# Two elementwise steps of an attention and feed-forward kernel on Pool instead of DVE

## The chip, the cores and the metric

The kernel runs on one core of one Trainium2 chip. The metric is device time in microseconds (us) of one execution; shorter is better. The engines of a core are named as the profile names them: PE multiplies matrices (PEld is its weight load), DVE and Pool (POOL) and ACT work elementwise, SP only issues DMAs here. Each engine takes its instructions in the order in which they stand in its own queue, and waits for the others through semaphores.

## What is computed

The first half is attention with a mask from hash buckets, for 4 batches of 8 heads, 768 positions, head size 64; the second half is a gated convolution with two matrix products, on the heads joined to 512 channels:

```python
q_bits = (einsum('bhsd,dk->bhsk', q, proj) > 0)          # 6 bits a position, k likewise
mask   = q_bucket[:, :, :, None] == k_bucket[:, :, None, :]
scores = where(mask, scale * (q @ k.T), -1e9)
attn   = softmax(scores)
x      = (attn @ v)  # heads joined: [4, 768, 512]
for k in range(5):
    gate_pre += conv_w[k] * xp[:, k:k + 768, :]           # xp: x with 4 zeros in front
out = (sigmoid(gate_pre) * (x @ w_val)) @ w_out
```

All arrays are fp32 (the weights of the second half arrive as 64-bit floats and are taken apart on the chip).

## The kernel before, in words

A unit is one head of one batch: 32 units. A tile is 128 queries of a unit against its 768 keys: 6 tiles a unit, 192 tiles in all. The main loop `for k in range(N + LAG + 1)` takes one tile a step and writes, by hand, the order in which each engine gets its work: PE, ACT, DVE and Pool run exactly in the order in which the code issues it (`tc.manual_schedule`), and SP's order follows from that.

For tile k, `scores` multiplies queries with keys on PE in two passes that add up: the first with operands rounded to the fp32r format (`aq`, `ak`), the second with the remainders (`bq`, `bk`). `maxima` takes the negated row maximum `nm` on DVE, `factors` and `shifts` make the two small columns `gs` and `nb`, and `exponentials` turns the scores to `p` on ACT with the row sums. For two tiles at a time `row_sums` and `recip` make the reciprocals `ri`, and `normalise` multiplies `p` with them on Pool. `transposes` (PE, tiles `tp`), `keep_transposed` (ACT, `pt`) and `attn_v` (PE, `av`) follow up to four steps later.

The raw queries and keys `r` of a unit lie stacked in one 128x768 tile. `prep` makes the four operands of the next unit, in two steps of the loop: first the rounding cast `aq<-r` (line 166), a step later the remainder `bq<-r,aq` on Pool (line 168) and six DMAs on SP's queue that place halves of `aq`, `bq` and the bit rows `u` in `ak`, `bk`, `bq` and `aq`. `stk` holds two buffers of each, so a unit is prepared while the one ahead is worked on.

When two heads (a pair, 128 channels) have their `x`, `pair_x` splits it in `xh` (DVE cast) and `xl` (Pool subtraction), and then runs the five taps of the convolution, one a call: tap 0 writes `g` (line 332), taps 1 to 4 add to it (line 334, DVE, two tensors in). Up to step 60 it is called every other step, after that every step. Four pairs end in the sigmoid on ACT and a `moe` generator for the two matrix products (PE lines 365 and 390, DVE lines 370 and 374, Pool line 376).

Over about the first 180 us two generators `load_weights` also take the 64-bit weights apart, eight pieces of 128x512, each some six DVE instructions (lines 92 to 108), two on Pool (110, 112), one on ACT (90) and a DMA.

Of the kernel before, what the change touches and what calls it, by code (L numbers as in the profile page):

```python
# [11 lines left out]
ALU = mybir.AluOpType  # L12
# [14 lines left out]
def kernel(  # L27
# [10 lines left out]
    nc = tc.nc  # L38
    B, H, _, S = qk.shape
# [103 lines left out]
    def load_raw(i):  # L143
        if i < len(units):
            b, h = units[i]
            raws[i] = raw.tile([P, S], FP32, name="r")
            nc.sync.dma_start(out=raws[i], in_=qk[b, h])

    def load_values(i):
        b, h = units[i]  # L150
        if h % 2 == 0:
            vts[i] = vp.tile([P, KB, P], FP32, name="vt")
            nc.sync.dma_start(out=vts[i], in_=v[b, h // 2])
        else:
            vts[i] = vts[i - 1]

    def prep(i):

        if i >= len(units):
            return  # L160
        b, h = units[i]
        j = h % 4
        load_values(i)
        r = raws[i]
        aq, ak, bq, bk = stacks[i] = [stk.tile([P, S], FP32R, name=nm) for nm in ("aq", "ak", "bq", "bk")]
        nc.vector.tensor_copy(out=aq, in_=r)  # L166
        yield
        nc.gpsimd.tensor_tensor(out=bq, in0=r, in1=aq.bitcast(FP32), op=ALU.subtract)  # L168
        nc.sync.dma_start(out=ak[0:D].bitcast(FP32), in_=aq[D:P].bitcast(FP32))
        nc.sync.dma_start(out=bk[0:D].bitcast(FP32), in_=aq[D:P].bitcast(FP32))  # L170
        nc.sync.dma_start(out=bk[D:P].bitcast(FP32), in_=bq[D:P].bitcast(FP32))
        nc.sync.dma_start(out=bq[D:P].bitcast(FP32), in_=aq[0:D].bitcast(FP32))
        u = cur["u"]
        nc.sync.dma_start(out=aq[D:M].bitcast(FP32), in_=u[32 * j:32 * j + 2 * NB].bitcast(FP32))
        nc.sync.dma_start(out=ak[D:M].bitcast(FP32), in_=u[32 * j + 2 * NB:32 * j + 4 * NB].bitcast(FP32))
        load_raw(i + 5)
        if j == 3 and i + 1 < len(units):
            yield
            yield from bits(i + 1)
# [6 lines left out]
    def bits(i):  # L186

        u = stk.tile([P, S], FP32R, name="u", bufs=2)
        for hf in range(2):
            yield  # L190
            sl = slice(hf * HS, (hf + 1) * HS)
            z = side_tile()
            for jj in range(4):
                nc.tensor.matmul(out=z[32 * jj:32 * jj + 32, 0:HS], lhsT=proj_sb,
                                 rhs=raws[i + jj][:, sl], start=True, stop=True,
                                 tile_position=(0, 32 * jj))
            nc.vector.tensor_scalar(out=u[:, sl], in0=z[:, 0:HS], scalar1=rows_sb[:, 0:1], scalar2=rows_sb[:, 1:2],
                                    op0=ALU.is_ge, op1=ALU.mult)
        cur["u"] = u
# [94 lines left out]
    def attn_v(i, pts):  # L294
        b, h = units[i]
        hh, c = h % 2, h // 2
        av = ps_v.tile([P, 512], FP32, name="av")
        vt = vts[i]
        for kb in range(KB):
            if kb:  # L300
                yield
            for s, pt in enumerate(pts):
                nc.tensor.matmul(out=av[s * D:(s + 1) * D, 0:HS], lhsT=vt[:, kb, hh * D:(hh + 1) * D], rhs=pt[kb // 3][:, kb % 3, :],  # L303
                                 start=(kb == 0), stop=(kb == KB - 1), tile_position=(0, s * D))
        if hh == 0:
            x = cur["x"] = xp.tile([P, S + KW - 1], FP32, name="x")
            nc.gpsimd.memset(x[:, 0:KW - 1], 0.0)
        x = cur["x"]
        for s in range(2):
            o = KW - 1 + s * HS  # L310
            nc.scalar.copy(out=x[hh * D:(hh + 1) * D, o:o + HS], in_=av[s * D:(s + 1) * D, 0:HS])  # L311
        if hh == 1:
            if c == 0:
                cur["xs"], cur["g"] = {}, []
            convs.append(pair_x(b, c, x, cur["g"], cur["xs"]))

    def pair_x(b, c, x, gs, xs_):
        for o in (0, HS):
            xh = xs.tile([P, HS], FP32R, name="xh")
            xl = xs.tile([P, HS], FP32R, name="xl")  # L320
            xs_[(c, o)] = (xh, xl)
            x0 = x[:, KW - 1 + o:KW - 1 + o + HS]
            nc.vector.tensor_copy(out=xh, in_=x0)  # L323
            nc.gpsimd.tensor_tensor(out=xl, in0=x0, in1=xh.bitcast(FP32), op=ALU.subtract)  # L324
        yield
        g = gp.tile([P, S], FP32, name="g")
        gs.append(g)
        for k in range(KW):
            yield
            w = cw_sb[:, c * KW + k:c * KW + k + 1]  # L330
            if k == 0:
                nc.vector.tensor_scalar(out=g, in0=x[:, 0:S], scalar1=w, scalar2=None, op0=ALU.mult)
            else:
                nc.vector.scalar_tensor_tensor(out=g, in0=x[:, k:k + S], scalar=w, in1=g, op0=ALU.mult, op1=ALU.add)  # L334
        if c == NP - 1:
            yield
            for g in gs:
                nc.scalar.activation(out=g, in_=g, func=AF.Sigmoid)
            cur["gates"] = 2
            moes.append(moe(b, xs_, gs))  # L340
# [101 lines left out]
    with tc.manual_schedule(engines=ENGINES):  # L442
# [3 lines left out]
        first_prep()  # L446
        weights = [[load_conv(), load_weights(0)], [load_weights(1)]]
        preps = [first_bits(), prep(1)]
        scores(0)
        step(weights[0])  # L450
        step(weights[1])
        turn = 0
        for k in range(N + LAG + 1):
# [15 lines left out]
            if k + 1 < N:  # L469
                if tiles[k + 1][0] != tiles[k][0]:  # L470
                    finish(preps)
                    preps = [prep(tiles[k + 1][0] + 1)]
                scores(k + 1)
# [83 lines left out]
```

## Time and profile before

| what | value |
|---|---|
| time, median of 3 runs | 639.09 us (638.87 to 639.24) |
| the profiled execution | 637.56 us, span of its instructions 635.6 us |
| PE busy | 590.1 us (93%) |
| DVE busy | 465.9 us (73%) |
| ACT busy | 421.7 us (66%) |
| POOL busy | 364.7 us (57%) |

Busy time of an engine is the time in which the profile shows an instruction running on it. The shares are means over a span with three stages: up to about 200 us the weights are taken apart and there is no feed-forward work for PE, then comes the long middle, and after 580 us only feed-forward products are left. In the rows, a group reads: line, engine, operation, output<-inputs, shapes, count, busy time and mean duration of one, then the time the engine idled just before them and what ended it.

### The profile page before, as it was taken

Reading aid. Unit: us, or ns where it says so; the run is one execution under the profiler, and the core shown is the slowest. Engines: PE = TensorE matmul, PEld = TensorE weight load, DVE = VectorE, ACT = ScalarE, POOL = GpSimd, SP = SyncE. Lnnn points to the kernel's source line nnn. Section 1 sums busy time; section 2 is a strip of 40 time slices with the busy share of each in tenths; the row PEclk is TensorE's granted clock in tenths of the full one; section 3 lists DMA queues with packets and bytes.
Section 4 is the critical chain, followed back from the end, with each engine's and each line's share of the span. In section 5 each row is a group of like instructions: output and inputs, shape, how many; then the busy total and the mean of one; then the engine's idle time right before and its main releaser. Section 6 shows DMA issues by size and latency. Waiting matters only on the chain.

```text
span 635.6 us, 10630 instructions
## 1 busy us (share of the span) xinstructions
PE 590.1 (93%) x3496; PEld 424.3 (67%) x3496; DVE 465.9 (73%) x1064; ACT 421.7 (66%) x881; POOL 364.7 (57%) x326
## 2 busy tenths in 40 slices
PE   4689888878999999999999999999999999999997
PEld 2465554555567777676667877677667777776895
DVE  5789897999986766668675877578685787665532
ACT  3487776767778666667787766677778677675400
POOL 1375868577765764567653776466562677544221
PEclk9899998998999999999999999999999999999999
DMA  6533535443332334343433333343422223300111
GB/s 243 128 101 86 139 96 138 112 134 81 104 80 58 83 75 123 82 105 96 104 80 79 88 80 110 80 121 80 120 57 61 57 53 79 86 18 2 50 51 50
DMA packets 23269, 56.76 MB, mean 89 GB/s; under 512 B 4296, under 2 KB 4296, under 8 KB 23216
## 3 DMA queue, kind: packets, MB, share of 16 engines
q1 hardware_dynamic: 23072, 56.06, 32.9%
q8 instruction: 28, 0.46, 0.3%
q14 instruction: 25, 0.20, 0.1%
q10 hardware_dynamic: 144, 0.03, 0.0%
HBM read 23.12 MB, written 6.29 MB: 46 GB/s over the span
## 4 chain that ended last, share of the span: by engine, by line
PE 64%; DVE 18%; ACT 10%; issue 3%; DMA 3%; POOL 0%; DVEq 0%; ACTq 0%
PE av L303 16%; PE s L232 15%; PE tp L280 12%; PE m L390 8%; PE m L365 7%; DVE nm L238 6%; ACT p L256 4%; DVE g L334 3%; ACT pt L289 3%; ACT x L311 2%; DMA w<-in_w_out_dram 2%; DVE aq L166 1%; PE tp L365 1%; PE tp L390 1%; PE s L390 1%
## 5 line engine op out<-in xcount | busy, mean ns | idle before, releaser
L271 POOL TENSOR_SCALAR p<-p,ri 128x768 f32<-128x768 f32 x192 | 220.0, 1150 | 200.3 <-DVE nb L248 157.6
L256 ACT ACTIVATE p<-s,nb,gs 128x768 f32<-128x768 f32 x192 | 192.7, 1004 | 49.7 <-DVE nb L248 44.6
L289 ACT COPY pt<-tp 128x384 f32<-128x384 f32 x384 | 166.2, 485 | 86.0 <-PE tp L280 85.0
L238 DVE TENSOR_REDUCE nm<-s 128x1 f32<-128x768 f32 x192 | 182.4, 950 | 52.8 <-PE s L232 52.6
L280 PEld LDWEIGHTS tp<-ident,p 128*128 128x128 f32 x1152 | 130.4, 142 | 74.2 <-issue 47.3
L280 PE MATMUL tp<-ident,p 128*128 128x128 f32 x1152 | 165.4, 280 | 4.5 <-ACT pt L289 1.6
L232 PE MATMUL s<-ak,aq 76*128 76x384 f32 x384 | 118.6, 390 | 32.2 <-ACT p L256 25.4
L303 PE MATMUL av<-pt,vt 128*64 128x384 f32 x768 | 146.9, 504 | 0.0
L232 PE MATMUL s<-bk,bq 128*128 128x384 f32 x384 | 101.6, 346 | 0.0
L232 PEld LDWEIGHTS s<-ak,aq 76*128 76x128 f32 x384 | 59.4, 195 | 48.9 <-ACT p L256 39.3
L303 PEld LDWEIGHTS av<-pt,vt 128*64 128x64 f32 x768 | 47.4, 137 | 63.3 <-issue 62.7
L334 DVE SCALAR_TENSOR_TENSOR g<-x,cw_sb,g 128x768 f32<-128x768 f32 x64 | 78.4, 1225 | 0.2
L232 PEld LDWEIGHTS s<-bk,bq 128*128 128x128 f32 x384 | 71.9, 194 | 0.5 <-issue 0.5
L376 POOL TENSOR_TENSOR hl<-ht,hh 128x384 fp32r<-128x384 f32 x32 | 33.4, 1044 | 45.5 <-DVE hh L374 45.5
L168 POOL TENSOR_TENSOR bq<-r,aq 128x768 fp32r<-128x768 f32 x31 | 58.4, 1885 | 0.5 <-DVE aq L166 0.5
L311 ACT COPY x<-av 64x384 f32<-64x384 f32 x64 | 30.4, 475 | 33.5 <-PE av L303 32.9
L365 PE MATMUL m<-xh,wv 128*128 128x384 f32 x200 | 42.7, 337 | 0.0
L248 DVE TENSOR_SCALAR nb<-nm,gs 128x1 f32<-128x1 f32 x192 | 40.1, 209 | 3.5
L370 DVE TENSOR_TENSOR ht<-m,g 128x384 f32<-128x384 f32 x25 | 13.9, 555 | 35.4 <-PE m L365 32.0
L256 ACT ACTIVATION_READ_ACCUMULATOR p<-s,nb,gs 128x1 f32 x192 | 39.1, 204 | 0.0
L324 POOL TENSOR_TENSOR xl<-x,xh 128x384 fp32r<-128x384 f32 x32 | 33.5, 1066 | 9.5 <-DVE xh L323 9.5
L390 PE MATMUL m<-wo,hh 128*128 128x512 f32 x144 | 38.1, 394 | 0.0
(84 smaller groups left out, 475.6 us busy)
## 6 DMA issues: line engine op xcount, KB each, us to landing
r<-in_qk_dram SPq DMA_DIRECT2D x32, 384.0 KB
vt<-in_v_dram SPq DMA_DIRECT2D x16, 384.0 KB
out_dram<-o SPq DMA_DIRECT2D x24, 256.0 KB
ak<-aq SPq DMA_DIRECT2D x31, 192.0 KB
bk<-aq SPq DMA_DIRECT2D x31, 192.0 KB
bk<-bq SPq DMA_DIRECT2D x31, 192.0 KB
bq<-aq SPq DMA_DIRECT2D x31, 192.0 KB
w<-in_w_val_dram SPq DMA_DIRECT2D x4, 512.0 KB
```

The lines of the kernel that those rows point to most:

```text
L168: nc.gpsimd.tensor_tensor(out=bq, in0=r, in1=aq.bitcast(FP32), op=ALU.subtract)
L232: nc.tensor.matmul(out=s[:, hf, 0:HS], lhsT=lq[0:n, qs], rhs=rk[0:n, hf * HS:(hf + 1) * HS], start=n == M, stop=n == P)
L238: nc.vector.tensor_reduce(out=nm, in_=s[:, :, 0:HS], axis=AX.XY, op=ALU.max, negate=True)
L256: nc.scalar.activation(out=p, in_=s[:, :, 0:HS], func=AF.Exp, bias=nb, scale=gs.pop(k), accum_out=sm[:, k % 2, 0:1])
L271: nc.gpsimd.tensor_scalar(out=p, in0=p, scalar1=rcs.pop(k), scalar2=1.0, op0=ALU.mult, op1=ALU.mult)
L280: nc.tensor.transpose(out=tp[:, n * P:(n + 1) * P], in_=p[:, kb * P:(kb + 1) * P], identity=ident)
L289: nc.scalar.copy(out=pt[:, :, qo:qo + P], in_=tp[:, 0:HS].rearrange("p (a b) -> p a b", b=P))
L303: nc.tensor.matmul(out=av[s * D:(s + 1) * D, 0:HS], lhsT=vt[:, kb, hh * D:(hh + 1) * D], rhs=pt[kb // 3][:, kb % 3, :], start=(kb == 0), s ...
L311: nc.scalar.copy(out=x[hh * D:(hh + 1) * D, o:o + HS], in_=av[s * D:(s + 1) * D, 0:HS])
L334: nc.vector.scalar_tensor_tensor(out=g, in0=x[:, k:k + S], scalar=w, in1=g, op0=ALU.mult, op1=ALU.add)
L365: nc.tensor.matmul(out=acc[:, 0:HS], lhsT=wv[wi][:, c, j * P:(j + 1) * P], rhs=xs_[(c, o)][xi], start=(m == 0), stop=(m == 11))
L390: nc.tensor.matmul(out=acc, lhsT=hs[(o, j)][hi][:, tb * P:(tb + 1) * P], rhs=wo[wi][:, j, :], start=(m == 0), stop=(m == 11))
```

## The change

The rounding cast `aq<-r` of every unit but the first (31 times, 128x768) and the first tap `g` of every pair (16 times, 128x768) are issued on Pool instead of DVE. On Pool the tap is a multiplication by the weight column and then by 1.0, which is the form that `normalise` has there.

```diff
-        nc.vector.tensor_copy(out=aq, in_=r)
+        nc.gpsimd.tensor_copy(out=aq, in_=r)
...
-                nc.vector.tensor_scalar(out=g, in0=x[:, 0:S], scalar1=w, scalar2=None, op0=ALU.mult)
+                nc.gpsimd.tensor_scalar(out=g, in0=x[:, 0:S], scalar1=w, scalar2=1.0, op0=ALU.mult, op1=ALU.mult)
```

The order on PE and ACT stays as it was. Below, `-` is a row of before, `+` one of now, and the brackets name the engines and DMA queues whose semaphores an instruction waits for.

DVE, at the place that the trace of before shows at 75 to 81 us (unit 5's cast, while the weight piece `w_848` is taken apart):

```order
 L92 TENSOR_SCALAR o<-o 128x512 [waits Activation_49]
 L93 TENSOR_SCALAR o<-o 128x512 [waits DVE_49]
-L166 CAST aq<-r 128x768 [waits DMAHW4_49,DMAHW1_49,DMAHW5_49,DMAHW0_49,Pool_49]
 L238 TENSOR_REDUCE nm<-s 128x1 [waits PE_49]
 L262 TENSOR_SCALAR s_973<-sm 128x2 [waits Activation_49]
```

The row maximum of the next tile now stands directly behind the weight's instruction. The first tap leaves DVE in the same way a few rows on, and the second tap, line 334, gets a wait for Pool.

Pool, at the same place (`p` is the normalising of a tile, `w_516` a weight piece):

```order
 L271 TENSOR_SCALAR p<-p,ri 128x768 [waits PE_49,Activation_49]
 L112 TENSOR_TENSOR wv_119<-w_516 128x512 [waits Pool_49]
-L271 TENSOR_SCALAR p<-p,ri 128x768 [waits DVE_49,PE_49,Activation_49]
-L168 TENSOR_TENSOR bq<-r,aq 128x768 [waits DMAHW1_49,PE_49]
-L271 TENSOR_SCALAR p<-p,ri 128x768 [waits PE_49,Activation_49]
+L166 CAST aq<-r 128x768 [waits DMAHW4_49,DMAHW1_49,DMAHW5_49,DMAHW0_49,PE_49]
+L271 TENSOR_SCALAR p<-p,ri 128x768 [waits DVE_49,Activation_49]
+L168 TENSOR_TENSOR bq<-r,aq 128x768 [waits PE_49,Pool_49]
+L271 TENSOR_SCALAR p<-p,ri 128x768 [waits PE_49,Activation_49]
+L332 TENSOR_SCALAR g<-x,cw_sb 128x768
 L307 MEMSET x 128x4
 L271 TENSOR_SCALAR p<-p,ri 128x768 [waits DVE_49,PE_49,Activation_49]
```

The cast stands ahead of the first `p` of a pair of tiles and waits for PE; the tap stands behind the second `p`.

Pool, at the start (unit 1, 19 to 25 us):

```order
 L271 TENSOR_SCALAR p<-p,ri 128x768 [waits DVE_49,Activation_49,Pool_49]
+L166 CAST aq<-r 128x768 [waits DMAHW2_49]
 L271 TENSOR_SCALAR p<-p,ri 128x768 [waits Activation_49]
-L168 TENSOR_TENSOR bq<-r,aq 128x768 [waits DMAHW2_49,DVE_49]
+L168 TENSOR_TENSOR bq<-r,aq 128x768 [waits Pool_49]
 L271 TENSOR_SCALAR p<-p,ri 128x768 [waits DVE_49,Activation_49]
```

Here the cast falls between two `p`, so that one of these stands between the cast and the remainder. On SP's queue some of the small DMAs `aq<-u` move ahead of the loads of `r` and `vt` that stood in front of them.

## The prediction

> **What bounds the kernel now.** The page's busy times (PE 93%, DVE 73%) are a mean over different programs, so I read them by stage, the weights' conversion apart. Columns: the stretch, its length, then PE, PEld, DVE, ACT, POOL busy (instructions), granted clock, DMA share, GB/s.
>
> ```profile
> 20.00:200.00 180.00, 156.03 (x934) 104.46 (x935) 159.85 (x357) 133.69 (x285) 120.84 (x105) 0.96 0.41 107
> 200.00:580.00 380.00, 373.22 (x2270) 273.37 (x2270) 272.13 (x651) 272.22 (x571) 226.43 (x202) 1.00 0.32 82
> 580.00:636.00 56.00, 50.47 (x257) 41.23 (x254) 22.58 (x35) 10.00 (x17) 14.00 (x14) 1.00 0.11 43
> ```
>
> From 200 to 580 us PE is idle for 6.8 of 380 us: whatever leaves DVE there can hardly shorten anything. From 20 to 200 us PE idles 24.0 us and DVE is the fullest engine, 159.85 of 180. There the chain of waits runs through DVE. Its shares from 20 to 200 us, and pieces in order of time (start, us, what), among them those that the change removes:
>
> ```profile
> by line: DVE nm L238 16.6%; PE s L232 9.1%; issue 7.9%; PE av L303 7.6%; DMA w<-in_w_out_dram 5.9%; ACT p L256 5.9%; DVE g L334 5.3%; PE tp L280 4.6%; DVE aq L166 4.3%; DVE w L100 3.5%; DVE nb L248 3.1%; ACT pt L289 2.6%; DVE gs L244 2.6%;
> ...
> 20.54 1.05 DVE aq L166
> ...
> 80.91 1.68 DVE g L332
> ...
> 94.17 0.47 DVE aq L166
> ...
> 103.52 6.17 DMA w<-in_w_out_dram
> ...
> 115.76 1.68 DVE g L332
> ...
> 139.55 4.47 DMA w<-in_w_out_dram
> ...
> 146.75 1.39 DVE aq L166
> ...
> 177.66 0.94 DVE aq L166
> 179.91 0.54 DVE g L332
> ```
>
> The casts are 4.3% of 180 us, 7.74 us in ten pieces, of which the fence has the first, the last and two between; the taps are the three shown, 3.90 us. Together 11.64 us of the chain.
>
> **The change part by part.** The groups that it moves, and those beside which they come to stand:
>
> ```profile
> L271 POOL TENSOR_SCALAR p<-p,ri 128x768 f32<-128x768 f32 x192 | 220.0, 1150 | 200.3 <-DVE nb L248 157.6
> L168 POOL TENSOR_TENSOR bq<-r,aq 128x768 fp32r<-128x768 f32 x31 | 58.4, 1885 | 0.5 <-DVE aq L166 0.5
> L166 DVE CAST aq<-r 128x768 fp32r<-128x768 f32 x31 | 20.6, 665 | 0.2
> L332 DVE TENSOR_SCALAR g<-x,cw_sb 128x768 f32<-128x768 f32 x16 | 13.2, 827 | 0.0
> ```
>
> DVE loses 33.8 us of work. Pool gains 16 taps in exactly the form of `p`, 1150 ns each, 18.4 us, and 31 casts. No row has a Pool cast. The bounds are `p` (one tensor in, one out) at 1150 and `bq` (two in, one out, same rounded type) at 1885 ns; I take `p`, because `bq` reads twice as much, and allow the other end: 36 to 58 us. So Pool goes to 419 to 442 us of 636, and it has 200.3 us of idle ahead of `p` alone.
>
> 1. *Removed from the chain, 20 to 200 us.* The first piece (1.05) does not count, see 3. That leaves 10.6 us. Where DVE would next wait for PE, the gain is given back:
>
> ```profile
> 177.14 0.62 PE L232 MATMUL s<-ak,aq 76*128 76x384 f32 x2 [0.25 <-ACT p L256]
> 118.94 0.85 PE L194 MATMUL m<-r,proj_sb 128*32 128x384 f32 x8
> 120.31 0.67 DVE L197 TENSOR_SCALAR u<-m,packed 128x384 fp32r<-128x384 f32 x1
> ```
>
> At 177 us PE has a gap of only 0.25 us, so of the last two pieces (1.48) about 0.5 remains. At 120 us DVE's `u` needs the product that ends at 119.8, 0.5 us ahead of it, while the tap just before gave 1.68: some 1.1 us is lost. Gain 10.6 - 1.0 - 1.1 = 8.5 us.
>
> 2. *The matmul clock.* Two long waits of PE in this stage are followed by slow matmuls (eight of `av` take 1.51 us elsewhere, as at 134.08):
>
> ```profile
> 97.17 0.62 PE L232 MATMUL s<-ak,aq 76*128 76x384 f32 x2 [2.16 <-ACT p L256]
> 98.36 2.83 PE L303 MATMUL av<-pt,vt 128*64 128x384 f32 x8
> 150.69 0.61 PE L232 MATMUL s<-ak,aq 76*128 76x384 f32 x2 [2.08 <-ACT p L256]
> 151.58 2.20 PE L303 MATMUL av<-pt,vt 128*64 128x384 f32 x8
> 133.19 0.61 PE L232 MATMUL s<-ak,aq 76*128 76x384 f32 x2 [2.21 <-ACT p L256]
> 134.08 1.51 PE L303 MATMUL av<-pt,vt 128*64 128x384 f32 x8
> ```
>
> Gaps of 2.16 and 2.08 us cost 1.32 and 0.69 us in `av`; one of 2.21 us cost nothing. The casts at 94.17 and 146.75 lie in the first two waits; without them those shrink. Of 2.0 us I take half, 1.0: the first is followed by a weight's DMA that does not come sooner for it.
>
> 3. *The start.* Unit 1's operands run in series: cast, `bq`, DMAs, first scores at 28.06. Now one more `p` stands between cast and `bq`:
>
> ```profile
> 19.35 1.83 POOL L271 TENSOR_SCALAR p<-p,ri 128x768 f32<-128x768 f32 x2 [12.12 <-DVE nb L248]
> 20.46 1.14 DVE L166 CAST aq<-r 128x768 fp32r<-128x768 f32 x1
> 21.68 1.80 POOL L168 TENSOR_TENSOR bq<-r,aq 128x768 fp32r<-128x768 f32 x1 [0.50 <-DVE aq L166]
> 28.06 0.98 PE L232 MATMUL s<-ak,aq 76*128 76x384 f32 x2 [2.31 <-issue]
> ```
>
> First `p` to about 20.3, cast to 21.3, second `p` to 22.2: `bq` starts at 22.2 instead of 21.68, a loss of 0.5 us. The DMAs on SP keep their order there.
>
> 4. *New collisions of DVE and Pool.* The two hold each other up, whole instructions long. The cast that met `L112` took 1.39 us, the one with Pool idle 0.55; line 334 beside `L110` took 1.85:
>
> ```profile
> 76.07 1.20 POOL L112 TENSOR_TENSOR wv<-w 128x512 fp32r<-128x512 f32 x1
> 76.30 1.39 DVE L166 CAST aq<-r 128x768 fp32r<-128x768 f32 x1
> 94.09 0.55 DVE L166 CAST aq<-r 128x768 fp32r<-128x768 f32 x1
> 161.83 1.31 POOL L110 TENSOR_TENSOR w<-w,wo 128x512 f32<-128x512 f32 x1
> 162.10 1.85 DVE L334 SCALAR_TENSOR_TENSOR g<-x,cw_sb,g 128x768 f32<-128x768 f32 x1
> L334 DVE SCALAR_TENSOR_TENSOR g<-x,cw_sb,g 128x768 f32<-128x768 f32 x16 | 21.0, 1312 | 0.0
> ...
> L334 DVE SCALAR_TENSOR_TENSOR g<-x,cw_sb,g x64: 1006/1009/2339, 86.8 to 596.0; 128x768 f32<-128x768 f32 x64
> ```
>
> The stage's 16 taps of line 334 average 1.31 us where an undisturbed one takes 1.01 (the last row: shortest, median, longest): 4.8 us lost beside 120.84 us of Pool work, 0.04 us per us, and I double that for DVE's other instructions. The stage gets 12 casts and 4 taps of 1.15 us, 18.4 us: 1.5 us. The far bounds are a gain of 1.5, should the collisions of the removed instructions have cost Pool as much, and a loss of 18.4 us, if each new one stops DVE for its whole length. I take 3.0 us, more than the mean rate, because the cast falls into the stretch where DVE goes from the maximum to the weights' two-tensor instructions.
>
> The Trainium skill ("SBUF — State Buffer", Who interferes with whom) says this as a rule: a DVE instruction in a two-port mode or with two SBUF inputs and a Pool instruction that reads SBUF take one pair of ports as an exclusive lock, and the second waits in full. The trace agrees (0.55 against 1.39 us). By the rule a Pool instruction that DVE runs into costs the rest of its length, half of 1.15 us on the mean: were all 16 run into, this term would be 9.2 us and the sum -0.3 instead of -6.5. "GPSIMD Engine Reference" (Engine selection) advises VectorE for elementwise work, calling Pool about twice as slow with two inputs and near line rate with one; 665 against 1150 ns (the latter for `p`) lies between.
>
> 5. *200 us to the end.* The casts (11.4 us) and taps lie beside PE. The chain has two casts there:
>
> ```profile
> 320.62 0.47 DVE aq L166
> 466.64 0.47 DVE aq L166
> ```
>
> The second tap now waits for Pool's first, but Pool has a step for it (192 tiles in 580 us: 3.0 us). With some collisions, net gain 0.5 us.
>
> 6. *SP.* The queue waits for the cast anyway, with the remainder behind it later still; both move with `p`, and the operands are due more than four steps on. The moved `aq<-u` DMAs cost nothing for the same reason. If that cover went, the scores of a new unit would wait.
>
> Sum: -8.5 - 1.0 + 0.5 + 3.0 - 0.5 = -6.5 us. Against the profiled execution, 637.56 us (span 635.6 and 1.96 around it), that is 631.1; this execution lies 1.5 us under the median of the runs, 639.09, so I forecast **632.6 us**.
>
> **The rivals.**
> - *A clean gain.* The collisions wash out (those of the removed instructions go as well) and both clock losses vanish: -10.6 - 2.0 + 0.5 = -12.1, 627.0 us. For it: Pool idles 200.3 us ahead of `p`, where the casts can lie while DVE reads scores from PSUM. Against it: the gap of 0.25 us, where PE is next.
> - *Given back.* At 103 and 139 us the chain hangs on weight DMAs of 6.17 and 4.47 us, and PE's three lines have 21.3% of it; if these set the stage's length, DVE's relief is idle time: 638.5 to 640 us. Against it: PE's 24 us of idle in the stage, DVE's 20.
> - *Slower: the lock.* One new Pool instruction ahead of the reciprocal or of a two-tensor instruction stops the column that ACT's next exponential waits for. At 1.0 us for each of the 16 the loss is 16.0 against a gain of 10.0 - 0.5: +6.5, 645.6 us. It decides from a mean of 0.6 us each; at half of 1.15 us each, 9.2 us in all, it takes the whole gain (638.8 us), which stands with the 0.10 of "given back" below. Against it: of 16 taps of line 334 the mean loss is 0.3.
> - *Slower: a Pool cast beyond `bq`'s price.* At 3 us, cast, two `p` and `bq` fill 7.2 us of the 6.0 us that two steps take, and transposes wait: about 1 us a unit after 200 us, where nothing hides it, 20 us, less the gain: 652 us. Only an unknown rate speaks for it; `bq`'s rounding output costs no extra against the fp32 row `L110` (1.31 us for 512, 1.885 for 768).
>
> **How the numbers follow.** A difference under 0.2%, 1.3 us, can't be told from none here. Forecast 0.63 (its own range 628.5 to 637.5), clean gain 0.12, given back 0.10, lock 0.11, slow cast 0.04. The range of 8 in 10 goes from 626.5, the clean gain with a little more, to 639.5: forecast, clean gain and most of "given back" are in. Faster 0.75, same 0.10, slower 0.15.
>
> **What would show it.** The stage ends with the first sigmoid:
>
> ```profile
> 196.31 3.05 ACT g L338 x4
> ```
>
> This should start 5 to 9 us sooner, and the rest of the span be as long as it was. DVE busy 432 to 436 us; a Pool cast of 0.9 to 1.9 us; `p` still idle by over 130 us. Line 334 at 1.2 to 1.4 us in the stage supports term 4; above 1.6 the lock wins. `av` at 1.51 us throughout supports term 2. First scores of unit 1 at 28.5 supports term 3. The forecast would be wrong if PE waits for Pool's `p` at every unit, if DVE's second tap waits for Pool's first, or if PE's waits for the exponential grow by what DVE lost.

## The result, and the profile after

| kernel | median of the runs | profiled execution |
|---|---|---|
| before | 638.98 us (637.55 to 639.24, 4 runs) | 637.56 us, span 635.6 |
| after | 632.10 us (631.53 to 632.61, 4 runs) | 632.0 us, span 629.8 |

The ratio is 0.9891 with a 95% interval of 0.987 to 0.9912: 7.0 us faster, 5.6 to 8.3 by the interval. The forecast was 632.6 us.

The page of after, its busy times over the whole span:

```profile
span 629.8 us, 10595 instructions
PE 588.4 (93%) x3496; PEld 424.0 (67%) x3496; DVE 446.7 (71%) x1017; ACT 421.3 (67%) x881; POOL 396.8 (63%) x373
```

DVE fell from 465.9 to 446.7 us, by 19.2 us, although 33.8 us of work left it. Added up by group, the durations of the instructions that stayed on DVE grew by 12.0 us; the rest of the 14.6 us that are missing is overlap, since busy time counts once where two records overlap. Pool rose from 364.7 to 396.8, and the prediction had 419 to 442.

The stages, cut where those of before were cut (columns as there: PE, PEld, DVE, ACT, POOL busy, granted clock, DMA share, GB/s):

```profile
20.00:200.00 180.00, 158.75 (x964) 107.26 (x960) 156.22 (x352) 137.83 (x292) 141.70 (x126) 0.97 0.42 110
200.00:580.00 380.00, 373.54 (x2275) 273.27 (x2275) 261.12 (x615) 271.26 (x571) 240.68 (x230) 1.00 0.32 81
```

The first sigmoid, with which the weights' stage ends, from ACT's order in time (start, us, what):

```profile
190.86 3.05 ACT L338 ACTIVATE g<-g 128x768 f32<-128x768 f32 x4
```

The sigmoid starts 5.45 us sooner (196.31 before). From there to the end it is 438.9 us, before 439.3. In the profiled executions 5.45 of the 5.8 us that the span lost thus lie ahead of 191 us. In the same 180 us PE now gets through 964 instructions, before 934. From 200 to 580 us PE is as full as it was, and DVE's 11 us less of work there buys next to nothing.

The chain of waits from 20 to 200 us, by line:

```profile
by line: DVE nm L238 14.1%; ACT p L256 10.3%; PE s L232 10.1%; PE av L303 8.8%; DVE g L334 5.9%; issue 4.6%; ACT pt L289 4.4%; PE tp L280 4.2%; DVE w L100 3.5%; DVE o L93 3.5%; DVE nb L248 3.0%; DMA w<-in_w_val_dram 3.0%; DVE w L96 2.6%; DM
```

The casts and first taps are gone from it, and the row, as far as it goes, has no line of Pool in their place. ACT's exponential has 10.3% instead of 5.9%, and its `pt` 4.4% instead of 2.6%: the round through ACT has gained a share. `L96`, a weight instruction that the row of before does not show, is on the chain with 2.6%.

The moved groups, line 334 and `av` (by line: shortest/median/longest in ns, first and last start):

```profile
L166 POOL CAST aq<-r x31: 816/824/1552, 20.2 to 533.4; 128x768 fp32r<-128x768 f32 x31
L332 POOL TENSOR_SCALAR g<-x,cw_sb x16: 902/907/1068, 82.6 to 587.0; 128x768 f32<-128x768 f32 x16
L334 DVE SCALAR_TENSOR_TENSOR g<-x,cw_sb,g x64: 1007/1202/2180, 85.4 to 591.1; 128x768 f32<-128x768 f32 x64
L303 PE MATMUL av<-pt,vt x768: 485/487/538, 39.0 to 583.2; 128*64 128x384 f32 x192
```

Two of the costliest groups of the page (count, busy us, mean ns, then idle before them and what ended it):

```profile
L271 POOL TENSOR_SCALAR p<-p,ri 128x768 f32<-128x768 f32 x192 | 212.4, 1110 | 165.6 <-DVE nb L248 149.5
...
L334 DVE SCALAR_TENSOR_TENSOR g<-x,cw_sb,g 128x768 f32<-128x768 f32 x64 | 83.3, 1302 | 2.2 <-POOL g L332 2.1
```

A Pool cast takes 0.82 us where nothing disturbs it and a tap 0.91: less than the 1.15 us that the prediction took from the mean of `p`, which holds its collisions. Pool still idles 165.6 us ahead of `p`. The median of line 334 rose from 1009 to 1202 ns. The longest `av` is 538 ns; before it was 903.

The eight weights' instructions of `L96` (two tensors in, 128x512), first before, then after, and from the order in time of after two of them with the Pool casts beside them:

```profile
L96 DVE SCALAR_TENSOR_TENSOR w<-w,o x8: 679/682/1308, 27.3 to 149.4; 128x512 int32<-128x512 int32 x8
```

```profile
L96 DVE SCALAR_TENSOR_TENSOR w<-w,o x8: 682/990/1308, 26.7 to 145.1; 128x512 int32<-128x512 int32 x8
```

```profile
91.57 1.55 POOL L166 CAST aq<-r 128x768 fp32r<-128x768 f32 x1
92.36 1.30 DVE L96 SCALAR_TENSOR_TENSOR w<-w,o 128x512 int32<-128x512 int32 x1
...
110.68 0.82 POOL L166 CAST aq<-r 128x768 fp32r<-128x768 f32 x1
111.06 0.99 DVE L96 SCALAR_TENSOR_TENSOR w<-w,o 128x512 int32<-128x512 int32 x1
```

This is a new collision in plain sight: where a Pool cast is under way, `L96` takes 0.99 to 1.30 us instead of 0.68 (one of the eight took 1.31 us before, too).

### The profile page after: what moved, and what is told of

Same layout as the page of the kernel before. It is cut to its first block, busy times and chain, and to the rows that moved or that the text cites. A ratio compares the mean times of both kernels' runs of the same rounds, so it can differ in the third digit from the quotient of the medians.

```text
span 629.8 us, 10595 instructions
## 1 busy us (share of the span) xinstructions
PE 588.4 (93%) x3496; PEld 424.0 (67%) x3496; DVE 446.7 (71%) x1017; ACT 421.3 (67%) x881; POOL 396.8 (63%) x373
## 4 chain that ended last, share of the span: by engine, by line
PE 66%; DVE 16%; ACT 13%; DMA 2%; issue 2%; POOL 0%; ACTq 0%; DVEq 0%
PE av L303 17%; PE s L232 16%; PE tp L280 12%; PE m L390 8%; PE m L365 7%; ACT p L256 6%; DVE nm L238 5%; ACT pt L289 4%; DVE g L334 3%; ACT x L311 2%; PE tp L365 1%; PE tp L390 1%; PE s L390 1%; DVE u L197 1%; DVE w L100 1%
## 5 line engine op out<-in xcount | busy, mean ns | idle before, releaser
L271 POOL TENSOR_SCALAR p<-p,ri 128x768 f32<-128x768 f32 x192 | 212.4, 1110 | 165.6 <-DVE nb L248 149.5
L303 PE MATMUL av<-pt,vt 128*64 128x384 f32 x768 | 145.0, 499 | 0.0
L334 DVE SCALAR_TENSOR_TENSOR g<-x,cw_sb,g 128x768 f32<-128x768 f32 x64 | 83.3, 1302 | 2.2 <-POOL g L332 2.1
```

What stands on the lines that cost most here:

```text
L271: nc.gpsimd.tensor_scalar(out=p, in0=p, scalar1=rcs.pop(k), scalar2=1.0, op0=ALU.mult, op1=ALU.mult)
```

## The experiments

The theories. A, the forecast's: DVE sets the pace in the weights' stage, the gain is the relief of it there, and the new collisions take a small part back. B: the gain goes by the amount of DVE work moved, wherever it lies. E: each new Pool instruction stops DVE for much of its length. A later rival is told where it stands.

In these kernels "early" means steps below 60 of the main loop (up to about 190 us): unit 1's cast, ten further casts and three first taps, so that 20 casts and 13 taps are late (two of the expectations count the fourth tap, near 180 us, as early). Each time is compared with runs of the kernel before on the same chip, whose medians lay between 638.2 and 639.0 us; microseconds of difference are worked out from the ratio.

**Each half alone.** Only the casts, and only the taps, on Pool:

```diff
-        nc.vector.tensor_copy(out=aq, in_=r)
+        nc.gpsimd.tensor_copy(out=aq, in_=r)
```

> Only the 31 casts run on Pool, the first taps stay on DVE. Theory A (the gain is DVE's time taken out of the chain of the first 200 us): chain pieces of the casts without the first 6.7 us, less about 0.5 given back, 1.0 from the matmul clock, a loss of 0.5 at the start and 2.2 from collisions: -4.5 us, 634.5 us. Theory B (what counts is DVE's freed busy time wherever it lies, 20.6 of 33.8 us): 61% of the 6.9 us, -4.2 us, 634.8 us, but with half of it after 200 us. The two differ here only in where the time goes: the first sigmoid under A comes 4 us sooner, under B 2 us.

Measured: 632.75 us, ratio 0.9912 (0.9899 to 0.9925), -5.6 us; the sigmoid at 191.24.

```diff
-                nc.vector.tensor_scalar(out=g, in0=x[:, 0:S], scalar1=w, scalar2=None, op0=ALU.mult)
+                nc.gpsimd.tensor_scalar(out=g, in0=x[:, 0:S], scalar1=w, scalar2=1.0, op0=ALU.mult, op1=ALU.mult)
```

> Only the 16 first taps run on Pool, the casts stay on DVE. Theory A: 3.9 us on the chain, 1.4 given back where PE or the bit rows are next, 0.8 of collisions: -1.7 us, 637.3 us. Theory B: 39% of 6.9 us, -2.7 us, 636.3 us. If taps and casts do not add up to the whole change, the two parts share a wait.

Measured: 637.01 us, 0.9985 (0.997 to 1.0001), -1.0 us, within what can't be told from nothing. The halves add up to -6.6 of the whole's -7.0. Their sizes do not decide between A and B (A had -4.5 for the casts, B -4.2), but the place does: with the casts alone the sigmoid comes 5.1 us sooner, where A had 4 and B 2.

**Each stage alone.** Both moves, early only and late only (the tap in the same way):

```diff
-        nc.vector.tensor_copy(out=aq, in_=r)
+        if cur["k"] < 60:        # late only: the branches exchanged
+            nc.gpsimd.tensor_copy(out=aq, in_=r)
+        else:
+            nc.vector.tensor_copy(out=aq, in_=r)
```

> Casts and first taps run on Pool only in the steps before 60 (11 casts, 4 taps, up to about 190 us); later ones stay on DVE. Theory A: the whole gain, 632 to 633 us. Theory B (gain wherever DVE is freed): 15 of 47 instructions and 15 of 34 us, about -3 us, 636 us. Theory C (the changes after 200 us cost time that the early ones hide): faster than the full change, 630 to 631 us.

> Casts and first taps run on Pool only from step 60 on (20 casts, 12 taps); early ones stay on DVE. Theory A: no difference to before, within 1 us of 639. Theory B: about -4 us, 635 us. Theory C: 640 to 641 us, slower.

Measured: early 632.45 us, 0.9911 (0.9896 to 0.9926), -5.7 us; late 637.55 us, 0.9987 (0.9978 to 0.9997), -0.8 us. The 14 early instructions carry the gain; the 33 late ones, with 19.9 of the 33.8 us of DVE's work, bring next to nothing. By amount of work (B) the late ones would bring the larger part.

**Unit 1's cast back on DVE**, the rest as in the change:

```diff
+        if i == 1:
+            nc.vector.tensor_copy(out=aq, in_=r)
+        else:
+            nc.gpsimd.tensor_copy(out=aq, in_=r)
```

> The changed kernel, but unit 1's cast back on DVE: on Pool a normalising instruction no longer stands between this cast and its remainder. Theory A: the start gets 0.5 us back, 631.6 us, first scores of unit 1 at 28.1 instead of 28.6. Rival: the start's gap is filled again before the second unit, no difference, 632.1 us.

Measured: 631.55 us, 0.9893 (0.9874 to 0.9912), the same as the change (0.9891). The start of Pool and of unit 1's first scores, before this kernel, then in the change:

```profile
21.66 1.81 POOL L171 TENSOR_TENSOR bq<-r,aq 128x768 fp32r<-128x768 f32 x1 [0.50 <-DVE aq L167]
28.47 0.98 PE L235 MATMUL s<-ak,aq 76*128 76x384 f32 x2 [1.43 <-ACT pt L292]
```

```profile
20.22 0.82 POOL L166 CAST aq<-r 128x768 fp32r<-128x768 f32 x1
21.02 0.91 POOL L271 TENSOR_SCALAR p<-p,ri 128x768 f32<-128x768 f32 x1
21.89 1.80 POOL L168 TENSOR_TENSOR bq<-r,aq 128x768 fp32r<-128x768 f32 x1
28.62 0.98 PE L232 MATMUL s<-ak,aq 76*128 76x384 f32 x2 [2.23 <-ACT p L256]
```

The first pair of rows is this kernel, the four below are the change. With the cast on DVE `bq` starts 0.23 us sooner, and the scores come only 0.15 us sooner, still 0.41 us behind before (28.06). Most of the late start is thus not the cast's. Other kernels say the same: with unit 1's cast on DVE the first scores start at 28.35 us in the ACT variant below and at 27.72 in the kernel with the late moves only; with it on Pool they start at 28.12 in the kernel with the casts alone.

**The new Pool work without the relief.** The kernel before with unused Pool copies of each cast and tap (the result, in bf16, goes to a tile that nobody reads), first at all 47 places:

```diff
         nc.vector.tensor_copy(out=aq, in_=r)
+        nc.gpsimd.tensor_copy(out=junk, in_=r)
```

> The kernel before, with its casts and first taps on DVE, and in addition, at the same places, a Pool cast of the same 128x768 input (31) and a Pool tap (16) whose results nobody uses. This measures what Pool's new instructions cost DVE without any relief of DVE. Theory A (collisions a modest price, 3.0 us, and 0.5 at the start): 2 to 5 us slower than before, 640 to 643 us. Rival D (collisions wash out): within 1 us of before. Rival E (each new Pool instruction stops DVE for about its length): 10 us or more slower, over 648 us; then DVE's relief is worth over 15 us, and not the 8.5 that the chain gave.

Measured: 645.51 us, 1.0111 (1.0093 to 1.0129), +7.1 us: more than the theory gave and less than the lock rival. The sigmoid starts at 201.38 us, 5.1 us late. Then only at the 13 early places (unit 1 excepted):

> The kernel before with an unused Pool cast and an unused Pool tap behind DVE's own at the 13 places ahead of step 60. It prices the new Pool instructions of the stage without any relief for DVE. Theory (collisions of about 0.15 to 0.3 us each on the path): +2 to +4 us over before, all of it ahead of the first sigmoid. Rival: each stops DVE for about half its length, +6 us or more. The kernel with all 47 extra instructions lost 6.9 us, 5.1 of them ahead of the sigmoid, with DVE's own cast and the extra one starting at the same moment; if the loss here is again about 5 us, that pair is what costs.

Measured: 643.13 us, 1.0078 (1.0062 to 1.0094), +5.0 us, the sigmoid at 202.40. That lies between the theory and its rival, near the 5 us that the expectation names last. A loss of this size does not by itself show that the pair costs it, so here are DVE's own casts and taps, first in the kernel before (25 to 178 us, without unit 1's cast), then in this one (20 to 190 us), and three groups of `av` of this one from PE's order in time:

```profile
L166 DVE CAST aq<-r 128x768 fp32r<-128x768 f32 x10 | 7.5, 753 | 0.0
L332 DVE TENSOR_SCALAR g<-x,cw_sb 128x768 f32<-128x768 f32 x3 | 5.3, 1766 | 0.0
```

```profile
L168 DVE CAST aq<-r 128x768 fp32r<-128x768 f32 x10 | 10.0, 1004 | 0.0
L338 DVE TENSOR_SCALAR g<-x,cw_sb 128x768 f32<-128x768 f32 x3 | 5.3, 1760 | 0.0
```

```profile
84.45 2.40 PE L308 MATMUL av<-pt,vt 128*64 128x384 f32 x8
...
119.67 2.13 PE L308 MATMUL av<-pt,vt 128*64 128x384 f32 x8
...
157.09 2.01 PE L308 MATMUL av<-pt,vt 128*64 128x384 f32 x8
```

DVE's casts average 1004 ns against 753 before, 2.5 us in all, while its taps are as long as before (1760 and 1766 ns). The 2.5 us come with the two copies of the same cast side by side, which the change does not have, because there the DVE copy is gone. And three groups of matmuls ran slow, against two before. So this kernel overprices the collisions of the change, by how much it cannot say.

**The relief without new Pool work.** The early casts (unit 1's excepted) and taps on ACT, all the rest as before:

```diff
+        if 1 < i and cur["k"] < 60:
+            nc.scalar.copy(out=aq, in_=r)
...
+                if cur["k"] < 60:
+                    nc.scalar.activation(out=g, in_=x[:, 0:S], func=AF.Copy, scale=w)
```

> Casts and first taps of the steps before 60 run on ACT (unit 1's cast stays on DVE), all others on DVE; Pool gets nothing new. It relieves DVE in the same way but without new Pool instructions. Theory A (relief 8.5 and clock 1.0, collisions gone, ACT with 46 us of idle in the stage): 629 to 631 us, faster than the change, unless ACT's order makes exponentials late. Rival F (the exponential is next on the chain, so 14 more instructions of 0.8 to 1.0 us on ACT come back in full): 636 to 640 us.

Measured: 630.31 us, 0.9869 (0.9853 to 0.9886), -8.4 us; the sigmoid at 189.06. `L96` keeps its median of 682 ns here:

```profile
L96 DVE SCALAR_TENSOR_TENSOR w<-w,o x8: 680/682/1290, 27.1 to 143.3; 128x512 int32<-128x512 int32 x8
```

ACT's groups of the moved work, 20 to 190 us:

```profile
L167 ACT CAST aq<-r 128x768 fp32r<-128x768 f32 x10 | 8.3, 828 | 0.0
L336 ACT ACTIVATE g<-x,cw_sb 128x768 f32<-128x768 f32 x3 | 2.8, 924 | 0.0
```

**The same, with the unused Pool copies beside it.** Here the operands do not go through Pool, so that what the Pool instructions cost is not a wait for their results:

```diff
+            nc.scalar.copy(out=aq, in_=r)
+            nc.gpsimd.tensor_copy(out=junk, in_=r)
```

> The ACT variant (630.3 us) with, in addition, an unused Pool cast and an unused Pool tap at the same 13 places ahead of step 60 at which the change has its own. Theory (collisions): what separates the change from the ACT variant is that its Pool instructions stop DVE's, so the unused ones give the difference back: about +2, 632 to 633 us, line 334 and the weights' DVE lines longer again, first sigmoid near 191 us. Rival (the way of the operands): the change is dearer only because the cast is on Pool's queue, ahead of the normalising and the remainder; unused instructions whose result nobody awaits then cost little, 630.3 to 631 us.

Measured: 632.22 us, 0.9911 (0.9896 to 0.9925), 2.7 us slower than the ACT variant by the ratios, 1.9 us by the medians (the intervals do not overlap), and exactly the ratio of the early half of the change. The sigmoid is back at 191.01, 1.95 us later than in the ACT variant. `L97` here is line 96 of the change; its group, two rows in order of time, and the taps that add (line 334 of the change) from 20 to 190 us:

```profile
L97 DVE SCALAR_TENSOR_TENSOR w<-w,o x8: 682/972/1317, 27.3 to 144.9; 128x512 int32<-128x512 int32 x8
```

```profile
91.31 1.55 POOL L169 CAST junk<-r 128x768 bf16<-128x768 f32 x1
92.11 1.30 DVE L97 SCALAR_TENSOR_TENSOR w<-w,o 128x512 int32<-128x512 int32 x1
```

```profile
L343 DVE SCALAR_TENSOR_TENSOR g<-x,cw_sb,g 128x768 f32<-128x768 f32 x16 | 20.1, 1257 | 0.0
```

The collisions of the weights' instruction return with the same durations to the hundredth (1.55 and 1.30 us), though nobody waits for these casts. So the operands' way is not the price. An unused cast could still hold up Pool's own queue, but behind eight of the ten Pool idles 0.66 to 4.31 us before its next `p`, and from 20 to 191 us PE waits for Pool's `p` once, for 0.6 us, in both kernels (its weight loads 5.2 us here and 6.2 in the ACT variant). Up to the sigmoid the durations of DVE's instructions add up to 2.2 us more than in the ACT variant, and the eight of `L97` alone to 2.0 us more (8.0 against 6.1). Line 334's growth in the change does not return with them (1257 ns against 1238 in the ACT variant and 1342 in the change).

**Both best parts together**: early on ACT, late on Pool.

> The ten casts and three first taps ahead of step 60 (unit 1's cast excepted, which stays on DVE) run on ACT, the 20 later casts and 13 later taps on Pool. If early and late parts add up, as they did on Pool (-5.8 and -0.7 us for -6.9 together), this is the ACT variant (-8.4 us against before) with another -0.7: -9.1 us, 629.5 us, with the first sigmoid at 189 us as in the ACT variant. Rival: late moves are worth nothing because PE is full there (or Pool then delays the operands of a unit), 630 to 631 us.

Measured: 630.09 us, 0.9875 (0.9861 to 0.9889), not told apart from the ACT variant: by the ratios and their intervals, from 1.0 us faster to 1.8 us slower. That is what the rival said, but the -0.8 of the late half still lies within it, so that this kernel does not settle whether late moves add. The profiled executions show no late gain: from the sigmoid to the end this kernel takes 439.1 us, the ACT variant 439.1, the late half alone 439.1, and before 439.3.

**How far relief of DVE goes.** The ACT variant with, in addition, the weights' casts, and then the casts of `x`, on ACT:

```diff
-            nc.vector.tensor_copy(out=hi, in_=a)
+            nc.scalar.copy(out=hi, in_=a)
```

> The ACT variant (630.3 us) with the eight rounding casts of the weights' pieces (line 108, 0.41 us each on DVE, 3.3 us in all) on ACT as well. Theory: in the stage DVE is still the engine that sets the pace, so relief of it is worth most of its size: -2 to -3 us, 627.5 to 628.5 us. Rival: with the casts and taps gone the pace is set by the round from scores through maximum, exponential and transposes back, and by ACT, so that the relief is idle time on DVE and the new ACT work delays exponentials: 630 to 631.5 us.

```diff
+            if cur["k"] < 60:
+                nc.scalar.copy(out=xh, in_=x0)
```

> The same with the eight casts of the pairs' x that lie ahead of step 60 (line 323, 0.52 us each on DVE, 4.2 us) on ACT too. If DVE sets the pace: another -2 to -3.5 us, 624.5 to 626.5 us. If the round through ACT does: no gain, 630 to 632 us, with PE's waits for the exponential as long as in the ACT variant or longer.

Measured: 630.88 us, 0.9884 (0.9868 to 0.99), and 632.26 us, 0.9905 (0.989 to 0.9921). Both times lie where the rival had them (the second 0.3 us above its range): DVE's busy time falls on, from 455.0 us in the ACT variant to 453.3 and 451.1, and nothing is gained; with both moves the kernel is slower than the ACT variant. The chain of the second (20 to 200 us) and its DVE waits from 20 to 190 us:

```profile
by line: ACT p L259 13.1%; PE s L235 10.1%; PE av L306 9.6%; DVE nm L241 9.3%; ACT pt L292 7.0%; issue 6.8%; PE tp L283 4.6%; DVE o L93 3.7%; DMA w<-in_w_val_dram 2.6%; DMA w<-in_w_out_dram 2.6%; DVE o L92 2.5%; DVE g L343 2.5%; DVE u L200 
DVE nm L241 <- PE s L235: 16.5, 19, 2.2
```

ACT's exponential heads the chain with 13.1%, and the maximum, at its head with 16.6% before, has 9.3%. DVE waits 16.5 us for scores where it waited 9.8 before. PE's waits for the exponential did not grow as the rival also said (15.6 us against 17.3 in the ACT variant). The chain points to the round from scores through the exponential to the transposes as what bounds the stage there. That is not shown: the chain of the kernel with unit 1's cast back on DVE, which is no faster than the change, has nearly the same shares (11.6% and 9.3%), and each of the two moves also puts its work on ACT. A further relief of DVE that loads no other engine was not run.

## Why the prediction was right, step by step

1. *Removed from the chain (-8.5) and 2. the matmul clock (-1.0).* Together -9.5 predicted, and -8.4 (7.3 to 9.4) by the ACT variant, which gives DVE the same relief but for unit 1's cast and one tap near 180 us, and puts 11 us on ACT. The place was right: 14 early instructions do it. Together the two terms were about 1 us too large. How the 8.4 divides between them is open, and so is how much of the missing 1 us is ACT's own extra work in the variant.

*The clock.* In the change and in the ACT variant the slow groups of matmuls are gone: `av` of the whole run took 146.9 us before and 145.0 in both, and the granted clock from 40 to 190 us is 1.00 in the change, where before it falls to 0.91 from 140 to 160 us. That looks like 1.9 of the 2.0 us of term 2, and `av` at 1.51 us is the sign that I had named for it. But the kernel with unit 1's cast back on DVE, as fast as the change, still has two slow groups (an undisturbed one takes 1.51 us):

```profile
95.36 0.83 PE L235 MATMUL s<-ak,aq 76*128 76x384 f32 x2 [1.68 <-ACT p L259]
...
96.76 2.61 PE L306 MATMUL av<-pt,vt 128*64 128x384 f32 x8
...
129.82 1.01 PE L235 MATMUL s<-ak,aq 76*128 76x384 f32 x2 [2.35 <-ACT p L259]
...
131.40 2.36 PE L306 MATMUL av<-pt,vt 128*64 128x384 f32 x8
```

Its `av` took 146.9 us, as before. PE waits less there instead: 12.3 us for the exponential from 20 to 190 us, against 17.9 in the change. The kernel with the early half alone has two slow groups as well (2.83 us each). So what term 2 is worth in time is not shown.

*The gap of PE as the cause of slow matmuls* was only a correlation in the trace of before (two gaps with, one without), and the casts that I put into those waits end 0.4 and 0.5 us ahead of them. After, gaps just as long stay harmless. PE's scores with the wait ahead of them (in brackets), and the next `av`, in the change:

```profile
130.27 0.62 PE L232 MATMUL s<-ak,aq 76*128 76x384 f32 x2 [2.37 <-ACT p L256]
131.16 1.51 PE L303 MATMUL av<-pt,vt 128*64 128x384 f32 x8
```

A gap of 2.37 us, longer than the 2.16 that went with 2.83 us of `av`, is followed by 1.51. In the kernel with both best parts a shorter one is followed by 2.83:

```profile
129.13 0.62 PE L237 MATMUL s<-ak,aq 76*128 76x384 f32 x2 [1.34 <-ACT p L261]
...
130.32 2.83 PE L308 MATMUL av<-pt,vt 128*64 128x384 f32 x8
```

So the length of a single gap is not what decides. Nor is it the sum of PE's waits for the exponential from 20 to 190 us: 19.9 us before and 12.3 in the kernel with unit 1's cast back on DVE go with two slow groups each, 17.9 after with none. What decides is open.

3. *The start (+0.5).* First scores at 28.62, where 28.5 was said, but not for the reason given: this was luck. Pool's `p`, cast and `p` took 0.90, 0.82 and 0.91 us, and `bq` started at 21.89 instead of 22.2. With the cast back on DVE the scores still come at 28.47, and the time is the same. `u`, whose DMA stands ahead of theirs on SP, started at 20.26 in the change and 20.32 in that kernel, 19.86 before: some 0.4 us late before unit 1's cast could matter. The term was nearly nothing.

4. *New collisions (+3.0).* Added to the ACT variant 13 instructions cost 2.7 us (1.9 by the medians), 0.2 us each, close to the term and far from the 0.6 from which the lock wins. The rule of the Trainium skill ("SBUF — State Buffer", Who interferes with whom) fits what a single pair does (`L96` at 1.30 instead of 0.68 us). As a price for all of them, half a length each, it was too high. Without relief, the same 13 instructions cost 5.0 us, part of it in pairs that the change does not have. Where I went wrong is DVE's busy time: 446.7 us, not 432 to 436. I had added no more than the 3.0 us of term 4; the durations of DVE's remaining instructions grew by 12.0 us over the whole run, 6.4 of it ahead of the sigmoid and the rest behind it, where the time hardly moved. Not all of it is new Pool work: in the ACT variant, which has none, they grew by 1.4 us ahead of the sigmoid. Line 334 in the stage stands at 1342 ns, in the range of 1.2 to 1.4, which says little: before (1312) and the ACT variant (1238) lie in it too.

5. *200 us to the end (-0.5).* The late half alone gave -0.8 (-1.4 to -0.2), and on top of the ACT variant nothing that could be told. PE's waits for the exponential from 200 to 570 us went from 3.9 to 3.0 us. The step holds within what can be measured.

6. *SP (0).* No run speaks against it: in after, PE waits for Pool's `p` once, for 0.6 us, as before.

The sum of what was measured, -8.4 + 2.7 - 0.8, is -6.5, the change itself -7.0; forecast was -6.5. The errors cancelled: terms 1 and 2 gave 1.1 us too much gain, and the start, the collisions and the late part were together 1.1 us too dear. That the sum came out so well is in part luck, since the measured parts have intervals of 0.6 to 1.4 us to either side.

The rivals: "given back" holds, if at all, only beyond the relief of the ACT variant. The lock is out with 0.2 us an instruction. The slow Pool cast is out at 0.82. Of the signs listed as proof against the forecast, one wait for Pool's tap appears, once and for 2.1 us (the group of line 334 above), in the part after 190 us, which did not get longer.

The lowest times are those of the ACT variant and of the kernel with both best parts, 630.3 and 630.1 us, 1.8 and 2.0 us below the change by the medians; the intervals of their ratios overlap that of the change, so that this lead is likely and not certain. The Trainium skill ("Perfetto Trace Analysis", Optimizing Scalar/DVE Operations) says that work moved from DVE to Pool might not help, as the two share a port. Here it helped by 7.0 us, and moving the early part to ACT helped by 8.4.

## What to carry to other kernels

Read a move between engines by stage: 14 of the 47 moved instructions, those in the stage where DVE was the fullest engine, brought most of the gain (5.7 of 7.0 us), and the other 33 little (0.8). The price of new work on an engine that shares something with the relieved one is measured best by adding it, unused, to a variant in which the relief is already there; added to the kernel before, it came out about twice as dear. And relief does not go on paying: the first 11 us of DVE's busy time (465.9 to 455.0) moved to ACT brought 8.4, the next 4 nothing; how much of that is the next round of waits, and how much ACT's own load, is open. Last, a trace of one execution tempts one to book what vanished from it as gain: the slow matmuls vanished from the change, and kernels just as fast have them.

## What the runs showed of the hardware

- A Pool cast from fp32 to fp32r, 128x768, takes 0.82 us undisturbed (start to start from the next `p` 0.80), a multiplication by a column 0.91, a subtraction of two tensors 1.80. ACT does the cast in 0.83 and the tap in 0.92, DVE in 0.55 and 0.61.
- DVE is held up beside Pool in very small instructions too. In the change, from 70 to 72 us (DVE's 128x2 instruction of line 262 beside two Pool subtractions), and the same instruction later:

```profile
70.32 1.96 POOL L324 TENSOR_TENSOR xl<-x,xh 128x384 fp32r<-128x384 f32 x2
71.35 0.95 DVE L262 TENSOR_SCALAR s<-sm 128x2 f32<-128x2 f32 x1
...
94.46 0.15 DVE L262 TENSOR_SCALAR s<-sm 128x2 f32<-128x2 f32 x1
```

  It takes 0.95 against 0.15 us, and the reciprocal of two tiles waits for it. The kernel before has the same at 71.43 us (0.96).
- Collisions lengthen both sides: the Pool cast at 91.57 took 1.55 us instead of 0.82, as DVE's line 334 was under way (90.89 to 92.44), and `L96` behind it then took 1.30.
- Slow groups of matmuls come in spells that cost PE about 1.6 us each. At 97.62 us before, the second pass of the scores took 0.81 instead of 0.53 us and the `av` behind it 2.83 instead of 1.51. From 80 to 160 us they followed waits of PE of 1.34 to 2.85 us in these kernels, and a wait of 2.37 us had none; the cause stays open.
